# One priority table, a single mask product and token mixing ahead of channel tiles in a blockwise-sparse attention + MLP-mixer kernel whose instruction order is planned at trace time

## The chip, the core and the metric

The kernel runs on one core of one Trainium2 chip. Its time is the device time of one execution in microseconds (us). A profiled execution is one run taken by the hardware profiler; its span runs from the first to the last instruction of the core.

## What is computed

Attention over 4 batches x 8 heads, 768 positions, head width 64, with a mask made of 32 x 32 blocks (neighbours, first and last block row and column, three drawn blocks per row); then a mixer layer over the 4 batches. Cut to what matters:

```python
scores = where(mask, q @ k.T / sqrt(64), -1e9)        # per batch and head, 768 x 768
attn   = softmax(scores) @ v                           # x: 4 x 768 x 512 (heads side by side)
h      = relu(x.T @ w_tok1) @ w_tok2                   # token mixing, 768 -> 256 -> 768
u      = x + h.T
out    = u + relu(u @ w_ch1) @ w_ch2                   # channel mixing, 512 -> 1536 -> 512
```

## The kernel before, in words

**Tiles.** Two heads form a pair; 16 pairs, four to a batch. A pair's 768 queries are cut into three thirds of 256 (index t), and each third has three key steps of 256 (index jj). One (p, t) is called a third here. For each step TensorE makes the transposed scores (line 764), ScalarE the exponential into the SBUF tile `et` (line 777), and TensorE multiplies the exponentials with the values (line 889), 24 matmuls a third, into one PSUM bank. A column of ones in the values gives the row sums; VectorE divides (lines 903 and 904) and writes `x`. The maximum is not subtracted.

**The mask.** In the first five pairs (`p < NT0`, NT0 = 5) 24 more contraction rows add a large negative number to masked scores: four matmuls of 88 rows a step. From pair 5 on the scores are made without it, two heads side by side in the array (64 rows each), 12 matmuls for a whole third, and VectorE multiplies the exponentials by a 0/1 mask (line 794). `CUTS` says how a third is cut for that: one product for steps 0 and 1, one for step 2.

**Getting q and k transposed.** Pairs 1 to 7 by TensorE (line 705), pairs 8 to 15 by DMA transposes from SyncE (line 665), both after loads that GpSimd issues (line 326).

**The mixer.** A batch's token mixing comes in two halves (two pairs each): 12 matmuls (line 970), a relu, 12 matmuls (line 992), three additions (line 1000), a DMA transpose of the sum (line 949). The first batch does it pair by pair, with TensorE transposes (lines 1024, 1046, 1068). Channel mixing: 96 matmuls a batch into 24 relus (lines 1104; 933 on ScalarE or 935 on VectorE), then 72 into six output rows (line 1132), each ended by an addition (line 1144) and a DMA to HBM.

**What sets the order.** Nothing is left to a scheduler. While the program is traced, class `Planner` plays all engines against a clock with assumed costs. TensorE's work comes as streams, each with a priority (lower goes first): scores 0, products with the values 1, transposes `TRP` = 2, the first batch's token mixing `TOKP` = 1.5, the other batches' token mixing 3, channel mixing 4. At each step the first stream whose inputs are there and whose PSUM bank is free emits one instruction. VectorE and ScalarE take from one list of waiting operations the ready one with the lowest `prio`: division 1, evacuations 0.9 or 2, relayouts 2 or 3, token sums and output sums 3, relu 4, mask product 5, exponentials 0. ScalarE leaves another operation alone if it would end more than `GRACE` after the next exponential can start. Engines run in program order, so an instruction that is placed too early blocks its engine.

**Banks.** PSUM has eight banks. In the later phase six belong to scores (three pairs), one (6) and one (7) to all else; `lend` says when a score bank may be lent: only if the time a borrower holds it (`HOLD`), is over before the next third's scores are expected, plus `LATER`.

**The clock.** `START` is the planner's time at the first scores; loads are planned on the same clock from constants.

Of the kernel before, what the change touches and what calls it, by code (L numbers as in the profile page):

```python
# [10 lines left out]
I32 = mybir.dt.int32  # L11
I64 = mybir.dt.int64
PLAN = False
AF = mybir.ActivationFunctionType
ALU = mybir.AluOpType

# [34 lines left out]
class Planner:  # L51
# [6 lines left out]


    PE_LAT, SEM = 180.0, 50.0  # L60
    GRACE = 0.0
    tight = 40e3
    trace = None

# [84 lines left out]
    def step(self):  # L149

        nxt = []
        moved = False
        if self.free_at["pe"] <= self.now:
            for s in self.streams:
                while s[3] is None or (callable(s[3]) and s[3]()):
                    s[3] = next(s[2], False)
                if s[3] is False or callable(s[3]):
                    continue
                cost, deps, tags, emit, done = s[3]
                t = self.when(deps, tags)  # L160
                if t is None:
                    continue
                if self.now < self.tight:

                    t += 300.0 if 1.5 < s[0] < 2.5 else 100.0 if s[0] == 1 else 0.0
                if t <= self.now:
                    s[3] = None
                    emit()
                    if self.trace is not None:
                        self.trace.append((self.now, "pe", s[0], cost))  # L170
                    self.free_at["pe"] = self.now + cost
                    if done is not None:
                        done.t = self.now + cost + self.PE_LAT + self.SEM
                    s[3] = next(s[2], False)
                    moved = True
                    break
                nxt.append(t)
            self.streams = [s for s in self.streams if s[3] is not False]
        else:
            nxt.append(self.free_at["pe"])  # L180
        for eng in ("act", "dve", "sp"):
            if self.free_at[eng] > self.now:
                nxt.append(self.free_at[eng])
                continue
            best, exp_at = None, 1e18
            if eng == "act":
                for o in self.ops:
                    if o[0] == 0 and o[2] == ("act",):
                        t = self.when(o[4], o[8])
                        exp_at = min(exp_at, 1e18 if t is None else max(t, self.now))  # L190
            for o in self.ops:
                prio, num, engines, cost, deps, emit, done, lat, tags = o
                if eng not in engines:
                    continue
                if eng == "act" and prio > 0 and self.now + cost["act"] > exp_at + self.GRACE:
                    continue
                t = self.when(deps, tags)
                if t is None:
                    continue
                if t <= self.now:  # L200
                    if best is None or (prio, num) < best[:2]:
                        best = o
                else:
                    nxt.append(t)
            if best is not None:
                prio, num, engines, cost, deps, emit, done, lat, tags = best
                self.ops.remove(best)
                emit(eng)
                c = cost[eng]
                if self.trace is not None:  # L210
                    self.trace.append((self.now, eng, prio, c))
                self.free_at[eng] = self.now + c
                done.t = self.now + c + lat + self.SEM
                moved = True
        if moved:
            return True
        later = [t for t in nxt if t > self.now]
        if not later:
            return False
        self.now = min(later)  # L220
        return True
# [3 lines left out]
def kernel(  # L225
# [20 lines left out]
    NV = 4  # L246
    NR = 4
    NET = 3
    NPE = 8
    NT0 = 5  # L250
    TOKP = 1.5
    TRP = 2

    sb1 = ctx.enter_context(tc.tile_pool(name="sb1", bufs=1))
    sbw = ctx.enter_context(tc.tile_pool(name="sbw", bufs=2))
# [256 lines left out]
    for hd in range(2):  # L512
        first_evac(vcopy, "k", 2, 4, hd, kt1)
    bandrows = free(indf[:, :], 0, [[0, 2], [1, S]])
    START = 5.7 * US
    P.now = START
    for eng in P.free_at:
        P.free_at[eng] = START
# [113 lines left out]
    def relayout(p):  # L632
        lays = {}
        for nm in ("k", "q", "v") if p >= NT0 else ("v",):
            raw = raws.pop((nm, p))
            arr = arrive.pop((nm, p))

            def emit(eng, nm=nm, raw=raw):
                if nm == "v":
                    nc.vector.tensor_copy(out=vaug[p % NV][:, :, :, 0:64], in_=raw)  # L640
                else:
                    lay = sbw.tile([128, NC, 2, D], BF16, tag=f"{nm}lay", bufs=2, name=f"{nm}lay{p}")
                    nc.vector.tensor_copy(
                        out=lay[:, :, :, :], in_=raw.rearrange("p h c d -> p c h d")
                    )
                    lays[nm] = lay

            deps = [arr]
            if nm == "v" and p >= NV:
                deps.append(pv_done[p - NV])  # L650
            if nm != "v" and p >= NT0 + 2:
                deps.append(qT_there[p - 2, 1])
            if nm != "v" and p >= NPE:
                deps.append(all_loaded)
            lays[nm + "ev"] = P.op(("dve",), {"dve": 320.0}, deps, emit, prio=2 if nm != "v" else 3)
            copied[nm, p] = lays[nm + "ev"]
        va_there[p] = lays["vev"]
        return lays
# [14 lines left out]
    def transposes(p):  # L673
# [15 lines left out]
        for nm, bufs, there in (("k", ktb, kT_there), ("q", qtb, qT_there)):  # L689
# [25 lines left out]
            if p >= NT0:  # L715
                def evac(eng, buf=bufs[p % NV], box=box):
                    copy = nc.scalar.copy if eng == "act" else nc.vector.tensor_copy
                    copy(out=buf[:, 0, :], in_=box["t"][:, :, :].rearrange("p c s -> p (c s)"))

                ev = P.op(  # L720
                    ("dve", "act"), {"dve": 555.0, "act": 740.0}, [last, mask_there], evac, prio=2
                )
                for hd in range(2):
                    alias(there[p, hd], ev)
                alias(rel, ev)
                continue
            for hd in range(2):
                def evac(eng, hd=hd, buf=bufs[p % NV], box=box):
                    i = box["t"][64 * hd : 64 * hd + 64, :, :].rearrange(
                        "p (h c) s -> p h c s", h=2  # L730
                    )
                    o = buf[0:64, :, :].rearrange("p h (c i s) -> p h c i s", c=3, i=2)[:, :, :, hd, :]
                    copy = nc.scalar.copy if eng == "act" else nc.vector.tensor_copy
                    copy(out=o, in_=i)

                ev = P.op(("dve",), {"dve": 550.0}, [last], evac, prio=0.9)
                alias(there[p, hd], ev)
                if hd == 1:
                    alias(rel, ev)

    def alias(a, b):
        a.same_as = b
# [9 lines left out]
    units = [(p, t) for p in range(NP) for t in range(3)]  # L752
    et_rel = {u: Ev() for u in units}
    VISIT = 3
    CUTS = ((0, 1), (2,))

    def scores(s, bank, done, rel, exps):
        p, t, jj = s
# [29 lines left out]
        for group in CUTS:  # L788
            if group[-1] != jj:
                continue  # L790

            def cut(eng, lo=group[0], n=len(group)):
                et = ets[p, t][:, lo : lo + n, :, :, :].rearrange("k j i h q -> k (j i) h q")
                nc.vector.tensor_tensor(  # L794
                    out=et, in0=et,
                    in1=free(mask[:, 2 * lo, 256 * t : 256 * t + 256], 0,
                             [[S, 2 * n], [0, 2], [1, 256]]),
                    op=ALU.mult,
                )

            ev = P.op(("dve",), {"dve": 158.0 + 537.0 * len(group)},
                      [exps[x] for x in group] + [mask_there], cut, prio=5)
            for x in group:
                alias(et_there[p, t, x], ev)

# [4 lines left out]
        return [k_first[int(jj > 0)], q_first[t], e2_first[t]]  # L810

    queue = deque(steps)
    UNSEEN, LATER = 2500.0, 1800.0
    HOLD = {"pm": 1600.0, "po": 1800.0, "ch1": 1800.0, "ch2": 4000.0}

    def lend(tag):
        if not queue:
# [54 lines left out]
    def pv_stream():  # L872
        for s in steps:
# [3 lines left out]
            def emit(s=s, done=done):  # L877
# [33 lines left out]
                        op=ALU.mult,  # L911
                    )

                ev = P.op(("dve",), {"dve": 610.0}, [done], norm, prio=1)
                alias(rel, ev)
                alias(x_there.setdefault((p, t), Ev()), ev)

# [41 lines left out]
    def tok(b, g):  # L959
        deps = [x_there[2 * g + 4 * b + i, h] for i in range(2) for h in range(3)] + [tok1_there]  # L960

        urgent = 3
        box = {}
        last, rel = Ev(), Ev()
        for t in range(2):
# [122 lines left out]
    def ch(b):  # L1088
# [4 lines left out]
        for cc in range(12):  # L1093
            for sh in range(2):
                last, rel, pbox = Ev(), Ev(), {}
                for dmc in range(4):
# [18 lines left out]
                    yield 162.5, deps, tags, emit, last if dmc == 3 else None  # L1115
                ev = relu_op(
                    lambda cc=cc, sh=sh: box["rc"][:, cc, 384 * sh : 384 * sh + 384],
                    pbox["pm"][:, 0:384], [last], 4,
                )
                alias(rel, ev)  # L1120
                rc_there[cc, sh] = ev
# [4 lines left out]
        for sc, lo, n in parts:  # L1126
# [30 lines left out]
                    in_=o[:, 0:n],  # L1157
                )

            alias(rel, P.op(("dve",), {"dve": dve_psum(n)}, [last], fin, prio=3))  # L1160
        alias(rc_rel, last)


# [27 lines left out]
    P.stream(TRP, tr_stream())  # L1191
    P.stream(TOKP, tok_first_stream(range(3)))
    P.stream(-1, tok_first_stream((3,)))
    P.stream(3, tok_stream((1, 2, 3)))
    P.stream(4, ch_stream())
    P.stream(1.8, mask_stream())

# [77 lines left out]
```

## Time and profile before

| what | us |
|---|---|
| median of 14 runs | 252.07 (251.58 to 257.71) |
| the profiled execution, as timed | 252.0 |
| its span | 250.3 |
| TensorE matmuls / VectorE / ScalarE / GpSimd busy | 242.4 / 164.7 / 176.5 / 49.4 |
| mask products: 33 of two steps, 33 of one step | 40.2 and 22.6 |
| exponentials, 144 | 137.1 |

The page gives one execution. "Busy" is the time in which an engine had at least one instruction under way; matmuls overlap their successors, so a matmul's own length (193 ns for one with 65 columns) is much more than the distance to the next (about 30 ns). For TensorE this text therefore reads distances between starts. An idle time is followed by what ended it, as in `<-DVE x`. The granted TensorE clock was 1.000 through the whole span.

### The profile page before, as it was taken

To read this page: it belongs to the slowest core of one execution; us is meant where nothing else is said; L and a number is where in the kernel's file an instruction comes from. 1 tells how busy PE (TensorE), PEld (TensorE's weight loads), DVE (VectorE), ACT (ScalarE), POOL (GpSimd) and SP (SyncE) were. 2 spreads that over 40 slices of the span, in tenths; PEclk is the share of its full clock that TensorE was granted. 3 is DMA by queue.
4 is the path that set the end of the run, shared out by engine and by line. 5 is a ranking of instruction groups with operands and counts; after the bars stand their busy time and mean duration, and the time that the engine had idled before them with its cause. 6 is when DMAs were issued, how large, how long until landed. Compare 5 with 4: busy or idle time off the path is not lost.

```text
span 250.3 us, 6580 instructions
## 1 busy us (share of the span) xinstructions
PE 242.4 (97%) x2788; PEld 163.0 (65%) x2807; DVE 164.7 (66%) x339; ACT 176.5 (71%) x225; POOL 49.4 (20%) x86
## 2 busy tenths in 40 slices
PE   8899999999999989999999999999999999999994
PEld 3689999966675557566765556666775665566444
DVE  5984885758697997988647687878795655200222
ACT  5999999998967777488669778589978820377000
POOL 8935888657600000000000000000000000000000
PEclk9999999999999999999999999999999999999999
DMA  7999999999976950663031452150006024300132
GB/s 163 162 219 202 203 207 201 205 201 203 199 119 120 169 133 24 92 162 65 0 65 34 74 87 63 47 148 0 3 0 65 3 84 93 138 3 0 42 118 94
DMA packets 42461, 26.35 MB, mean 105 GB/s; under 512 B 23680, under 2 KB 38800, under 8 KB 42432
## 3 DMA queue, kind: packets, MB, share of 16 engines
q0 software_dynamic: 15104, 12.98, 33.0%
q1 hardware_dynamic: 26784, 12.56, 22.7%
q8 instruction: 22, 0.36, 0.6%
q10 hardware_dynamic: 544, 0.39, 0.5%
q14 instruction: 7, 0.06, 0.1%
HBM read 26.74 MB, written 6.29 MB: 132 GB/s over the span
## 4 chain that ended last, share of the span: by engine, by line
PE 88%; DMA 4%; POOL 3%; DVE 2%; issue 1%; ACT 1%; POOLq 0%
PE banks L1132 25%; PE banks L1104 24%; PE banks L764 15%; PE banks L889 13%; DMA w_tok<-in_moe_w_tok_dram 4%; PE banks L970 3%; PE banks L992 3%; PE banks L705 1%; PE banks L1024 1%; PE banks L1046 1%; POOL vraw L326 1%; POOL kraw L326 1%; POOL qraw L326 1%; PE banks L1068 1%; ACT et L777 1%
## 5 line engine op out<-in xcount | busy, mean ns | idle before, releaser
L777 ACT ACTIVATE et<-banks 128x1024 bf16<-128x1024 f32 x144 | 137.1, 1024 | 24.5 <-PE banks L764 24.0
L1132 PE MATMUL banks<-w_ch,rc 128*128 128x512 bf16 (+2 forms) x293 | 67.7, 362 | 2.2 <-DVE x L904 1.0
L1104 PE MATMUL banks<-uT,w_ch 128*128 128x384 bf16 x384 | 68.5, 326 | 0.0
L794 DVE TENSOR_TENSOR et<-et,mask 128x2048 bf16<-128x2048 bf16 x66 | 61.2, 952 | 3.2 <-ACT et L777 3.1
L764 PE MATMUL banks<-qtb,ktb 64*128 64x256 bf16 (+1 forms) x576 | 54.3, 271 | 0.4 <-ACT et L777 0.4
L889 PEld LDWEIGHTS <-et 128*128 128x128 bf16 x1152 | 45.7, 97 | 10.2 <-DVE et L794 2.1
L889 PE MATMUL banks<-vaug,et 128*128 128x65 bf16 x1152 | 50.3, 193 | 0.3
L933 ACT ACTIVATE rc<-banks 128x384 bf16<-128x384 f32 x71 | 34.4, 495 | 23.0 <-PE banks L1104 22.4
L1104 PEld LDWEIGHTS <-w_ch 128*128 128x128 bf16 x384 | 35.7, 98 | 22.1 <-issue 1.3
L1132 PEld LDWEIGHTS <-rc 128*128 128x128 bf16 x312 | 27.7, 97 | 27.6 <-issue 3.5
L764 PEld LDWEIGHTS <-ktb 64*128 64x128 bf16 (+1 forms) x576 | 31.9, 95 | 15.2 <-issue 12.1
L1144 DVE TENSOR_TENSOR o<-banks,x 128x512 f32<-128x512 f32 x23 | 15.8, 687 | 30.7 <-PE banks L1132 30.6
L903 DVE RECIPROCAL recip<-banks 128x4 f32<-128x4 f32 x48 | 8.7, 181 | 27.8 <-PE banks L889 26.6
L904 DVE TENSOR_TENSOR x<-banks,recip 128x256 bf16<-128x256 f32 x48 | 20.4, 424 | 1.7
L935 DVE TENSOR_SCALAR rc<-banks 128x384 bf16<-128x384 f32 x25 | 13.8, 554 | 7.3 <-PE banks L1104 7.1
L1000 DVE TENSOR_TENSOR x<-banks,x 128x512 bf16<-128x512 f32 x18 | 11.4, 683 | 3.1 <-PE banks L992 3.1
L970 PE MATMUL banks<-x,w_tok 128*128 128x256 bf16 x72 | 10.0, 273 | 0.0
L992 PE MATMUL banks<-a_t,w_tok 128*128 128x256 bf16 x72 | 9.2, 273 | 0.3 <-DVE a_t L935 0.3
L992 PEld LDWEIGHTS <-w_tok 128*128 128x128 bf16 x72 | 7.9, 126 | 0.9 <-issue 0.4
L970 PEld LDWEIGHTS <-w_tok 128*128 128x128 bf16 x72 | 6.6, 98 | 2.4 <-issue 0.8
L326 POOL DMA_DIRECT2D vraw<-in_v_dram x10 | 7.4, 742 | 2.5 <-DVE recip L903 1.2
L326 POOL DMA_DIRECT2D kraw<-in_k_dram x9 | 6.6, 729 | 4.3 <-DMA w_tok<-in_moe_w_tok_dram 2.7
(94 smaller groups left out, 132.3 us busy)
## 6 DMA issues: line engine op xcount, KB each, us to landing
out_dram<-o SPq DMA_DIRECT2D x23, 256.0 KB, 2.0
w_ch<-in_moe_w_ch_dram POOLq DMA_DIRECT2D x8, 384.0 KB, 9.8
vraw<-in_v_dram POOLq DMA_DIRECT2D x10, 192.0 KB, 7.3
kraw<-in_k_dram POOLq DMA_DIRECT2D x9, 192.0 KB, 8.8
qraw<-in_q_dram POOLq DMA_DIRECT2D x9, 192.0 KB, 7.3
w_tok<-in_moe_w_tok_dram POOLq DMA_DIRECT2D x2, 384.0 KB, 10.8
qf<-in_v_dram POOLq DMA_DIRECT2D x4, 192.0 KB, 7.8
klay_first<-in_k_dram POOLq DMA_DIRECT2D x2, 192.0 KB, 8.3
```

What stands on the lines that cost most here:

```text
L326: nc.gpsimd.dma_start(out=raw, in_=APx(src, 2 * p * S * D, [[NC * D, 128], [S * D, 2], [1, NC * D]]),)
L764: nc.tensor.matmul(out=ps[:, hd, 256 * i : 256 * i + 256], lhsT=ktb[n][rows, h, 256 * jj + 128 * i : 256 * jj + 128 * i + 128], rhs=qtb[n] ...
L777: nc.scalar.activation(out=ets[p, t][:, jj, :, :, :].rearrange("k i h q -> k h i q"), in_=ps.rearrange("k h (i q) -> k h i q", i=2), func= ...
L794: nc.vector.tensor_tensor(out=et, in0=et, in1=free(mask[:, 2 * lo, 256 * t : 256 * t + 256], 0, [[S, 2 * n], [0, 2], [1, 256]]), op=ALU.mult,)
L889: nc.tensor.matmul(out=po[:, hd, c, :], lhsT=et[:, jj, i, hd, 128 * c : 128 * c + 128], rhs=va[:, hd, 2 * jj + i, 0:65], start=(jj == 0 an ...
L904: nc.vector.tensor_tensor(out=free(xs[b][:, pb // 2, 2 * t, 128 * (pb % 2) : 128 * (pb % 2) + 128], 0, [[64, 2], [256, 2], [1, 64]],), in0 ...
L933: nc.scalar.activation(out=o(), in_=i, func=AF.Relu)
L970: nc.tensor.matmul(out=box["pm"][:, t, :], lhsT=w_tok1[:, sc, 128 * t : 128 * t + 128], rhs=xs[b][:, g, sc, :], start=(t == 0 and sc == 0) ...
L992: nc.tensor.matmul(out=ubox["pm"][:, i, :], lhsT=w_tok2[:, t, :, 2 * s2 + i], rhs=a_t[:, t, :], start=(i == 0 and t == 0), stop=(i == 1 an ...
L1104: nc.tensor.matmul(out=pbox["pm"][:, 0:384], lhsT=w_ch1[:, dmc, 128 * cc : 128 * cc + 128], rhs=st[b]["uT"][:, dmc // 2, 3 * sh : 3 * sh + ...
L1132: nc.tensor.matmul(out=pbox["pm"][:, 0:n], lhsT=box["rc"][:, cc, 128 * sc : 128 * sc + 128], rhs=w_ch2[:, cc, lo : lo + n], start=(cc == 0 ...
L1144: nc.vector.tensor_tensor(out=o[:, :].rearrange("p (g e) -> p g e", g=2), in0=pbox["pm"][:, :].rearrange("p (g e) -> p g e", g=2), in1=st[ ...
```

## The change

All numbers of the planner are put into one table `KN` and several are different; one of them picks another cut for the mask product. The diff, cut to its core:

```diff
+KN = dict(
+    tokp=2.5, trp=2.6, toks=1.2, later=1400.0, unseen=1500.0, h_pm=1200.0, h_po=1800.0,
+    h_ch1=1400.0, h_ch2=3500.0, relayk=0.8, relayv=4.6, fin=2.1, relu=0.85, cut=5.0, norm=0.6,
+    add=3.0, ev2=2.0, ev4=3.3, grace=400.0, m1=0.0, m2=150.0, nt0=5, cuts=2, xbar=8,
+)
-    GRACE = 0.0
+    GRACE = KN["grace"]
-                    t += 300.0 if 1.5 < s[0] < 2.5 else 100.0 if s[0] == 1 else 0.0
+                    t += KN["m2"] if s[0] == KN["trp"] else KN["m1"] if s[0] == 1 else 0.0
-    TOKP = 1.5
-    TRP = 2
+    TOKP = KN["tokp"]
+    TRP = KN["trp"]
-    START = 5.7 * US
+    START = 6.5 * US
-    CUTS = ((0, 1), (2,))
+    CUTS = (((0,), (1,), (2,)), ((0, 1), (2,)), ((0, 1, 2),), ((0,), (1, 2)))[KN["cuts"]]
-    UNSEEN, LATER = 2500.0, 1800.0
-    HOLD = {"pm": 1600.0, "po": 1800.0, "ch1": 1800.0, "ch2": 4000.0}
+    UNSEEN, LATER = KN["unseen"], KN["later"]
+    HOLD = {tag: KN["h_" + tag] for tag in ("pm", "po", "ch1", "ch2")}
-    P.stream(3, tok_stream((1, 2, 3)))
+    P.stream(KN["toks"], tok_stream((1, 2, 3)))
```

The `prio` numbers of VectorE's and ScalarE's operations are read from the table in the same way: relayouts of q and k 2 to 0.8, of v 3 to 4.6, evacuations 0.9 to 2.0 and 2 to 3.3, division 1 to 0.6, relu 4 to 0.85, output sum 3 to 2.1; token sums (3) and mask product (5) stay. The mask product of a third becomes one operation over three steps. NT0 and the number of pairs transposed by TensorE are the same numbers as before. Nothing that is computed changes, and TensorE's instructions are the same in number and kind; their order is not.

## The prediction, made before the changed kernel ran

> **What bounds the kernel now.** I read the page's busy shares first, then the chain that ended last, then TensorE's timeline.
>
> ```profile
> PE 242.4 (97%) x2788; PEld 163.0 (65%) x2807; DVE 164.7 (66%) x339; ACT 176.5 (71%) x225; POOL 49.4 (20%) x86
> ...
> PE 88%; DMA 4%; POOL 3%; DVE 2%; issue 1%; ACT 1%; POOLq 0%
> ```
>
> TensorE carries 88% of the chain. The Trainium skill (Perfetto Trace Analysis, "Identifying the Most-Contended Engine") warns that matmul busy share doesn't show how near a kernel is to its bound, and says to take weight-load busy share: here 65%, which would leave a third of the span, some 85 us, to be had by a better order. The trace decides, by distances between starts. The chain in order of time has
>
> ```profile
> 100.85 2.16 PE banks L1132 x10
> ...
> 123.52 1.31 PE banks L992 x12
> ...
> 215.95 15.60 PE banks L1104 x96
> ```
>
> (start, length, what), so 0.216, 0.109 and 0.1625 us a matmul. A third's 12 scores take 0.86 with the step into them, 24 value products 0.73 (0.0305 each), a step of the first five pairs 0.436, a small transpose or first-batch token matmul 0.056. Sum: 45 x 0.436 + 33 x 0.86 + 1152 x 0.0305 + 384 x 0.1625 + 288 x 0.216 + 2.65 (the last row's small pieces) + 144 x 0.109 + 204 x 0.056 = 237.4 us. From the first scores (6.18) to the last matmul (247.2) are 241.0 us. So TensorE is full; only some 3 us are idle, and no order can win more. That is the ceiling, not 85.
>
> Where are they? I compared, from one third's scores to the next, the elapsed time with the work in between. Most of the 32 intervals agree within 0.02 us. One that doesn't:
>
> ```profile
> 88.98 0.83 PE L764 MATMUL banks<-qtb,ktb 64*128 64x256 bf16 x12
> 89.74 0.60 PE L1132 MATMUL banks<-w_ch,rc 128*128 128x512 bf16 x2
> 90.18 0.89 PE L889 MATMUL banks<-vaug,et 128*128 128x65 bf16 x24
> 91.80 0.81 PE L1132 MATMUL banks<-w_ch,rc 128*128 128x512 bf16 x2 [0.73 <-DVE x L904]
> 92.54 0.83 PE L764 MATMUL banks<-qtb,ktb 64*128 64x256 bf16 x12
> ```
>
> Value products started at 90.18 end after 0.73 at 90.91; the next channel row waits until the division has freed their bank, at 91.80: 0.89 idle (one of its three matmuls is missing in the record). By the same sum: 0.49 from 96.19 (relu of a token half), 0.22 from 102.94, 0.09 from 109.86, 0.43 from 113.65 (mask product), 0.46 from 138.24 (division), 0.12 in two others. **Together 2.7 us after pair 5 has begun.** The other waits are in the first 19 us.
>
> **One mask product instead of two.**
>
> ```profile
> L794 DVE TENSOR_TENSOR et<-et,mask 128x2048 bf16<-128x2048 bf16 x33 | 40.2, 1219 | 3.2 <-ACT et L777 3.1
> ...
> L794 DVE TENSOR_TENSOR et<-et,mask 128x1024 bf16<-128x1024 bf16 x33 | 22.6, 685 | 0.0
> ```
>
> Two steps take 1219 ns, one 685: 534 a step and 151 fixed. Three steps then take 1.75 us (an estimate from these rows; at least that, at most the 1.90 of both). VectorE saves 33 x 0.151 = 5.0 us. In the new order 16 more channel relus are VectorE's (41 for 25, 554 ns each: +8.9), so its busy time rises to about 168 us, and ScalarE loses 16 x 0.495 = 7.9. Neither sets the end, so both count nothing by themselves.
>
> What counts is that the values must wait longer. From the start of a third's scores: 0.49 to the first exponential (134.49 to 134.98), 2.85 for three, 0.05, product, 0.1. Before, the last step was ready after 0.49 + 2.85 + 0.05 + 0.69 + 0.1 = 4.2 us, now all of it after 5.24. Here the skill speaks against the change: Perfetto Trace Analysis, "Optimizing Scalar/DVE Operations", says that grouping pays where the engine is saturated, and that where VectorE isn't but makes others wait, operations should be broken up. VectorE is at 66%. By the rule, with values where they were (TensorE work between scores and values 4.4 to 4.9 us in some 20 thirds), each would wait some 0.6: +12 us. By the new order it doesn't: values come later too. Summing TensorE's work between scores and values at the prices above gives 5.32 to 5.49 us in ten thirds, 5.5 to 9.6 in the others. All cover 5.24, ten with a margin of only 0.08 to 0.25. I take the order's sum.
>
> **The new priorities and lending.** The order shows what they do after pair 5: a third's 24 values run unbroken (before, mostly 16 and 8 with channel work between); 24 of 48 accumulators for values lie in lent score banks (5 before), so channel rows wait less for a division. Unbroken or not, they cost the same: 0.73. I went through the places of the new order where an instruction follows closely on what frees its bank or makes its input. None of the old waits is left, two new ones are. (a) Values of pair 12, second third: after the last of 12 token matmuls TensorE has 4 channel rows' matmuls, scores, 6 token and 1 channel matmul, 0.86 + 0.86 + 0.65 + 0.22 = 2.6 us; VectorE in that time ends a division (0.65), the token relu (0.69) and the product (1.75), 3.1 to 3.2 with hand-over: 0.5 idle. (b) Pair 7, last third: three products stand in VectorE's queue with an output sum and a division between; 0.2 short. Cost 0.7; the bounds are 0.3 (the old waits were often shorter than such a sum) and 1.2.
>
> SyncE's queue: the transpose of batch 1's first half moves ahead of pair 8's q and k (1.3 us each). Those land by about 81 us and are read at 90: hidden. Batch 1's second half is read about 5.6 us after its issue; the row of such a transpose shows 5.2 to landing: covered by 0.4, up to 0.4 more if SyncE is late. GpSimd's loads are the same in number, with some homes exchanged from pair 5 on, and nothing ahead of them changed. The last was issued at 67.3, landed some 8 us later and is read after 110, so this costs nothing.
>
> So after pair 5: -2.7 + 0.7 = -2.0 us.
>
> **START and the first token matmul.** This part loses. `START` moves the planner's scores 0.8 us later against its own estimate of loads, so it believes loads to be there sooner relative to TensorE's work.
>
> ```profile
> 17.77 0.60 PE L764 MATMUL banks<-qtb,ktb 88*128 88x256 bf16 x4
> 18.21 0.41 PE L889 MATMUL banks<-vaug,et 128*128 128x65 bf16 x8
> 18.83 0.40 PE L1024 MATMUL banks<-x,w_tok 128*128 128x128 bf16 x4 [0.21 <-DMA w_tok<-in_moe_w_tok_dram]
> ...
> DMA to landing us min/median/max: 9.9/9.9/9.9
> ```
>
> The first token weights (issued at 8.93, landing after 9.9) come at 18.83, and the first matmul that reads them waits for just that. No load ahead of them changes, so they will again. In the new order one such matmul stands ahead of a score step and 16 values that now run ahead of it: 0.436 + 0.488 = 0.92 us. TensorE gets there at about 17.8 (also after new waits for pair 1's q, landing at 10.28, and pair 2's k, at 13.4, which this wait swallows), stands until 18.83, and has 0.92 us of work more ahead than before. From 20 to 49 us TensorE shows no wait for ScalarE, so nothing absorbs it: **+0.9 us** (bounds 0.2, if ScalarE's queue turns out to rule there, and 1.0).
>
> **Sum.** -2.0 + 0.9 = -1.1 against the profiled execution's 252.0 (span 250.3 and 1.7 around it): span 249.2, time 250.9. The median before, 252.07, is the same within 0.1.
>
> **Rivals.**
> - The early delay is absorbed, because exponentials and TensorE are nearly balanced in the first 50 us (ScalarE 98% busy from 20 to 50). Then 250.9 - 0.9 = 250.0. Against it: no idle on TensorE there. 0.13.
> - Idle is only moved: new waits of 1.2 to 2.2 us that my sums miss, at transposes and in bank hand-overs, together with the early 0.9 give 251.4 to 252.4. This is also the case that the table doesn't do what it says, as relus go to VectorE. 0.22.
> - Slower: the long product starts late. VectorE is in the middle of a relu or sum (0.55 to 0.69) when the third exponential ends; nothing can overtake, and the values stand at the head of TensorE's queue. With lateness 0.3 in the ten tight thirds and the five next (margin 0.3) the shortfalls add to 1.0, nearly the whole gain; with 0.4 to 2.4: 253.3. It decides from about 0.3 on. For it: VectorE gets the 16 relus; against: in the new order the product follows right on the last exponential in most thirds. 0.12.
>
> **How the numbers follow.** Likeliest 0.53: 250.9, of its own 250.2 to 251.6. A measurement of this kernel can tell about 0.3% from no change, 0.76 us: faster is below 251.3. That is most of the likeliest case, and all of the first rival: 0.66. Same 0.22, slower 0.12. The range, 249.8 to 252.4, takes in the first rival, most of the second and the bounds of the waits, and leaves out the slow one.
>
> **What would show it.** TensorE idle about 1.0 us before 18.83 with the token weights as releaser, and the score step after it at about 18.9; pair 5's first scores near 54.1 as before, with 6 fewer channel matmuls ahead of them (0.97 us, which hides the delay there); from there to the last batch's 96 channel matmuls 2 us less idle, those starting near 214.9 (before 215.95); the product at about 1750 ns x33; waits of channel rows for the division gone. Wrong would be: products above 1.9 us, TensorE idle before values in more than five thirds, or a first-token wait that doesn't move the later starts.

## The result, and the profile after

| | before | after |
|---|---|---|
| median, us (runs) | 252.13 (48, with those shown above) | 250.56 (10, 249.98 to 251.25) |
| ratio, 95% interval | | 0.9939 [0.9924, 0.9955] |
| profiled execution, as timed / span | 252.0 / 250.3 | 250.6 / 248.9 |

The change gains 0.6%, 1.6 us. Ratios, here and below, take the undisturbed executions alone, against the kernel before as timed on the same chip. The page of the kernel after, busy shares, chain and the groups that the change touches (the changed kernel's line numbers are 5 or 6 higher):

```profile
PE 242.1 (97%) x2788; PEld 163.1 (66%) x2807; DVE 170.3 (68%) x321; ACT 170.1 (68%) x210; POOL 49.7 (20%) x86
...
PE 90%; ACT 4%; DMA 2%; DVE 1%; issue 1%; SPq 0%; DVEq 0%
...
L1138 PE MATMUL banks<-w_ch,rc 128*128 128x512 bf16 (+2 forms) x293 | 65.7, 362 | 1.1 <-issue 0.2
L800 DVE TENSOR_TENSOR et<-et,mask 128x3072 bf16<-128x3072 bf16 x33 | 57.8, 1752 | 1.7 <-ACT et L783 1.5
...
L941 DVE TENSOR_SCALAR rc<-banks 128x384 bf16<-128x384 f32 x41 | 22.2, 553 | 5.3 <-PE banks L1110 4.3
```

The three-step product takes 1752 ns, 33 times, and 41 channel relus are VectorE's. TensorE's busy time stands where it stood. The list of what TensorE waited for is short now (waiting line, releaser: us in all, times, longest):

```profile
PE banks L469 <- ACT qlay_first L461: 1.0, 1, 1.0
PE banks L394 <- DVE one L387: 1.0, 1, 1.0
PE banks L770 <- ACT et L783: 0.3, 1, 0.3
PE banks L1138 <- issue: 0.2, 1, 0.2
```

Before, it had channel rows waiting for the division (1.0 us) and token products for a relu (0.3). Both are gone, and no wait for another engine after pair 5 is named in their place. The list is not complete: the comparison of starts, as in the prediction, finds two places more, 0.45 us in pair 12 and 0.12 in pair 9 (shown further below). TensorE's timeline in pair 12 (start, length):

```profile
154.31 0.83 PE L770 MATMUL banks<-qtb,ktb 64*128 64x256 bf16 x12
155.07 0.64 PE L998 MATMUL banks<-a_t,w_tok 128*128 128x256 bf16 x4
155.54 0.38 PE L1138 MATMUL banks<-w_ch,rc 128*128 128x512 bf16 x1
155.87 0.38 PE L998 MATMUL banks<-a_t,w_tok 128*128 128x256 bf16 x2
156.36 0.90 PE L895 MATMUL banks<-vaug,et 128*128 128x65 bf16 x24
```

Two token matmuls need 0.22, so the values at 156.36 start 0.27 later than TensorE could. A further 0.11 lies ahead of the token matmuls at 155.87; what caused it was not settled. VectorE at the same time:

```profile
153.62 0.42 DVE L910 TENSOR_TENSOR x<-banks,recip 128x256 bf16<-128x256 f32 x1
153.96 0.68 DVE L941 TENSOR_SCALAR a_t<-banks 128x512 bf16<-128x512 f32 x1
154.56 1.75 DVE L800 TENSOR_TENSOR et<-et,mask 128x3072 bf16<-128x3072 bf16 x1
```

Division, token relu, product, one behind the other: the product ends at 156.31, and the values follow at 156.36. These 0.27 are wait (a) of the prediction. The chain of waits, in order of time, has near its end

```profile
214.59 15.60 PE banks L1110 x96
```

The last batch's 96 channel matmuls start at 214.59, before at 215.95: 1.36 sooner, the whole difference of the spans (1.4).

**Two numbers that split every run.** One is the start of the last score step of the first five pairs, TensorE's 45th: it tells how late the front is. Before it was at 49.00, after at 49.73. The other is TensorE's idle time after pair 5: from pair 5's first scores to the last third's, the elapsed time less the work in between at the prediction's prices. Before it was 2.85, after 0.76. So the front lost 0.73 and the rest gained 2.09: 250.3 + 0.73 - 2.09 = 248.9, the span measured. All runs of the study, split in this way:

| run | median, us | ratio, 95% interval | 45th step | idle after pair 5 | sum | span |
|---|---|---|---|---|---|---|
| before | 252.13 | | 49.00 | 2.85 | | 250.3 |
| before again | 251.68 | 0.9999 [0.9984, 1.0015] | 48.97 | 2.85 | 250.3 | 250.3 |
| after | 250.56 | 0.9939 [0.9924, 0.9955] | 49.73 | 0.76 | 248.9 | 248.9 |
| after again | 250.81 | 0.9953 [0.9937, 0.9969] | 50.01 | 0.76 | 249.2 | 249.2 |
| after, START 5.7 | 250.9 | 0.9962 [0.9946, 0.9977] | 49.38 | 0.76 | 248.6 | 248.6 |
| after, token weights planned later | 250.03 | 0.9932 [0.9920, 0.9945] | 49.10 | 0.77 | 248.3 | 248.3 |
| after, two products | 255.48 | 1.0149 [1.0124, 1.0173] | 48.93 | 5.99 | 253.4 | 253.4 |
| before, one product | 255.65 | 1.0150 [1.0132, 1.0167] | 48.60 | 5.96 | 253.0 | 253.9 |
| after, old lending | 251.8 | 0.9992 [0.9973, 1.0012] | 49.66 | 1.98 | 250.1 | 250.1 |
| before, new priorities | 252.69 | 1.0027 [1.0007, 1.0047] | 49.36 | 2.46 | 250.3 | 250.3 |
| the same and GRACE | 253.49 | 1.0061 [1.0044, 1.0078] | 49.54 | 3.51 | 251.5 | 251.5 |
| the same and one product | 251.74 | 1.0001 [0.9978, 1.0025] | 49.70 | 1.98 | 250.1 | 250.1 |
| after, GRACE 0 | 264.13 | 1.0493 [1.0443, 1.0543] | 49.37 | 9.47 | 257.3 | 259.9 |
| after, two edits | 250.33 | 0.9933 [0.9900, 0.9965] | 50.18 | 0.48 | 249.1 | 249.1 |

The sum is 250.3 plus the differences of both columns from before. It meets the span within 0.1 in all but two runs: with one product in the kernel before, 0.9 lies behind the last third's scores; with GRACE at 0, 2.6, of which 2.40 is a wait of the last batch's channel matmuls for a transpose. The two columns lie in stretches that don't overlap, so the two parts of the prediction can be judged apart. They say nothing of the time outside the span: with the new priorities alone the span is that of the kernel before, but 2.0 us of the profiled execution (252.31) lie outside it, for 1.7 before.

### The profile page after: what moved, and what is told of

It is laid out like the page before. It is cut to its first block, busy times and chain, and to the rows that moved or that the text cites. A ratio compares the mean times of both kernels' runs of the same rounds, so it can differ in the third digit from the quotient of the medians.

```text
span 248.9 us, 6575 instructions
## 1 busy us (share of the span) xinstructions
PE 242.1 (97%) x2788; PEld 163.1 (66%) x2807; DVE 170.3 (68%) x321; ACT 170.1 (68%) x210; POOL 49.7 (20%) x86
## 4 chain that ended last, share of the span: by engine, by line
PE 90%; ACT 4%; DMA 2%; DVE 1%; issue 1%; SPq 0%; DVEq 0%
PE banks L1110 26%; PE banks L1138 24%; PE banks L770 16%; PE banks L895 13%; ACT et L783 4%; PE banks L976 3%; PE banks L998 3%; DMA qf<-in_q_dram 2%; PE banks L711 1%; PE banks L1052 1%; PE banks L1030 1%; DVE et L800 1%; PE banks L1074 1%; ACT qlay_first L461 0%; PE banks L469 0%
## 5 line engine op out<-in xcount | busy, mean ns | idle before, releaser
L1138 PE MATMUL banks<-w_ch,rc 128*128 128x512 bf16 (+2 forms) x293 | 65.7, 362 | 1.1 <-issue 0.2
L800 DVE TENSOR_TENSOR et<-et,mask 128x3072 bf16<-128x3072 bf16 x33 | 57.8, 1752 | 1.7 <-ACT et L783 1.5
L895 PEld LDWEIGHTS <-et 128*128 128x128 bf16 x1152 | 43.6, 97 | 6.6 <-issue 1.1
L895 PE MATMUL banks<-vaug,et 128*128 128x65 bf16 x1152 | 46.7, 193 | 0.1
L939 ACT ACTIVATE rc<-banks 128x384 bf16<-128x384 f32 x55 | 26.8, 492 | 22.1 <-PE banks L1110 21.6
L941 DVE TENSOR_SCALAR rc<-banks 128x384 bf16<-128x384 f32 x41 | 22.2, 553 | 5.3 <-PE banks L1110 4.3
L976 PE MATMUL banks<-x,w_tok 128*128 128x256 bf16 x72 | 9.5, 273 | 0.1
L615 POOL COPY mask<-maskb 128x240 bf16<-128x240 bf16 (+1 forms) x18 | 7.4, 478 | 0.0
```

The lines of the kernel that those rows point to most:

```text
L800: nc.vector.tensor_tensor(out=et, in0=et, in1=free(mask[:, 2 * lo, 256 * t : 256 * t + 256], 0, [[S, 2 * n], [0, 2], [1, 256]]), op=ALU.mult,)
L895: nc.tensor.matmul(out=po[:, hd, c, :], lhsT=et[:, jj, i, hd, 128 * c : 128 * c + 128], rhs=va[:, hd, 2 * jj + i, 0:65], start=(jj == 0 an ...
L939: nc.scalar.activation(out=o(), in_=i, func=AF.Relu)
L941: nc.vector.tensor_scalar(out=o(), in0=i, scalar1=0.0, scalar2=None, op0=ALU.max)
L976: nc.tensor.matmul(out=box["pm"][:, t, :], lhsT=w_tok1[:, sc, 128 * t : 128 * t + 128], rhs=xs[b][:, g, sc, :], start=(t == 0 and sc == 0) ...
L1138: nc.tensor.matmul(out=pbox["pm"][:, 0:n], lhsT=box["rc"][:, cc, 128 * sc : 128 * sc + 128], rhs=w_ch2[:, cc, lo : lo + n], start=(cc == 0 ...
```

## The experiments

The theory that stood after the result: after pair 5 the gain comes from the order that all parts of the table make together, and the front's loss is real and hidden by nothing. Rivals: one part alone (priorities, merge, lending, GRACE) makes the gain; the front's loss comes from the first token matmul, as predicted, or from how the first loads happen to land. Each expectation stands as it was put on record before its run.

**Both kernels again**, without an edit, show what repeats.

> The kernel before, unchanged, for a second trace of its first 20 us and of its idle time. If the loads at the start vary from run to run, the first token matmul starts at another time than 18.83 us or the second part of q arrives at another time than 6.3 us, while the idle time of TensorE after pair 5 stays at 2.7 to 2.9 us, since the order is fixed. If the idle time after pair 5 is chance, it differs by more than 0.5 us. Time 252.0.

> The changed kernel, unchanged. Theory: idle time of TensorE from pair 5's first scores to the last third's is 0.8 us as in its first trace (0.45 of it before the values of pair 12, second third). The early delay depends on when the first token weights land: at 18.8 us they cost 0.9, at 16.6 nothing. Rival: the 1.0 us by which q's second part came later in the first trace belongs to the change, and is seen again here. Time 250.6 by the theory with early weights, 251 with late ones.

Measured: idle after pair 5 repeats to 0.01 us (2.85 and 2.85, 0.76 and 0.76). The front does not: the 45th step came 1.04 later in this pair of profiles, 0.73 in the first. In the second profile of the changed kernel TensorE stands in the front at another place:

```profile
11.14 0.51 PE L711 MATMUL banks<-ident,qraw 128*128 128x128 bf16 x6 [0.83 <-DMA qraw<-in_q_dram]
11.48 0.60 PE L770 MATMUL banks<-qtb,ktb 88*128 88x256 bf16 x4
```

Pair 1's q landed at 11.1 (10.3 in the first profile), and its transposes now stand ahead of a score step, pair 0's fifth. In the kernel before that score step came first.

**START back.**

```diff
-    START = 6.5 * US
+    START = 5.7 * US
```

> The changed kernel with START = 5.7 again. From pair 4 on its order is that of the changed kernel; before that pair 1's q and pair 2's k are turned later, and the first token matmul stands behind a score step and 16 values as in the kernel before. If START costs 0.9 us by the wait for the first token weights, this is 0.9 faster than the changed kernel where they land at 18.8 and 0 to 0.2 faster where they land at 16.6. If the earlier turning of q and k fills idle time of TensorE near 9 to 12 us (its rival), START = 6.5 is a gain and this is 0.5 to 0.8 slower.

Measured: 250.9, as good as the changed kernel's 250.81 on the same chip; idle after pair 5 again 0.76. The order after pair 4 is the same. From the fifth score step to the 45th it takes 39.33, with START at 6.5 38.50; the fifth step comes sooner in exchange (10.05). By these medians and the equal idle time, START is not what made the gain, and not what lost the front.

**The planner believes the first token weights 0.9 us later**, so that the first token matmul stands behind one more score step and 16 values.

```diff
-        tok1_there.t = landing(t, S * DT * 2).t
+        tok1_there.t = landing(t, S * DT * 2).t + 900.0
```

> The changed kernel, with the planner's arrival of the first token weights put 0.9 us later, and nothing else. Early turning of q and k stays; the first token matmul moves behind a score step and 16 values. From pair 4 on the order is that of the changed kernel. If the wait for those weights costs, 0.9 faster than the changed kernel with weights at 18.8, the same with weights at 16.6. If the early delay is all q's late part, the same in any case.

Measured: the first token matmul moved from 18.23 to 18.93, and from the fifth score step to the 45th it takes 38.57 for 38.50. So its place cost nothing, with the weights landing at 16.66 and 17.70 in the two. The front was 0.6 sooner than in the changed kernel's profile because this run's first loads landed sooner (below). The median, 250.03, is lower than the changed kernel's, but the intervals overlap.

**One part undone or done alone: the cut of the product.** The changed table with the old cut, then the old kernel with the new cut:

```diff
-    ... nt0=5, cuts=2, xbar=8,
+    ... nt0=5, cuts=1, xbar=8,
```

> The changed kernel with two mask products a third again (cuts=1), all else as changed. If the merge itself pays (one fixed cost of 0.15 us less a third), this loses little, 0 to 1 us, and half of the gain after pair 5 stays. If the breaking-up rule is right here, it is faster than the changed kernel. My theory: the planned order fits only its own set of numbers; places in its order where channel rows and value accumulators follow closely on an output sum or a division add to 4 to 6 us of idle time after pair 5 against 0.8: time 253.5 to 255.5.

```diff
-    CUTS = ((0, 1), (2,))
+    CUTS = ((0, 1, 2),)
```

> The kernel before with one mask product a third and nothing else. If the merge carries the gain, 250.5 to 251.5. By my theory it alone costs: the values come later, bank hand-overs then meet the output sums, and the places in its order add to about 5 us of idle time after pair 5 against 2.8, and one transposed token half is read too early at the end (up to 1.3): time 254 to 255.5. Without any move of the values by the planner it would be 264.

Measured: both lose 1.5%, with idle times of 5.99 and 5.96. In the changed table with two products, values wait 1.4 us in one place, and channel rows 1.6 us in three, for an output sum on VectorE. The old order with the long product pays at pair 9 for what the rule cited in the prediction would break up (TensorE's timeline):

```profile
107.99 0.40 PE L764 MATMUL banks<-qtb,ktb 64*128 64x256 bf16 x4 [0.47 <-ACT et L777]
108.90 0.40 PE L764 MATMUL banks<-qtb,ktb 64*128 64x256 bf16 x4 [0.52 <-ACT et L777]
110.70 1.50 PE L889 MATMUL banks<-vaug,et 128*128 128x65 bf16 x24 [1.40 <-DVE et L794]
112.01 2.30 PE L1104 MATMUL banks<-uT,w_ch 128*128 128x384 bf16 x7
```

Scores wait for exponentials to free their banks, then the values wait 1.40 for the product. Counted from start to start, these waits make only 2.7 of the 4.39 us lost there. The 24 values then take 1.31 to the next start instead of 0.73, and the channel matmuls behind them run slowly too. The table by windows (length, PE, PEld, DVE, ACT and POOL busy, granted TensorE clock, DMA share, GB/s) says why:

```profile
107.00:110.70 3.70, 1.31 (x14) 0.52 (x13) 2.36 (x2) 3.70 (x6) 0.00 (x0) 0.99 1.05 224
110.70:114.00 3.30, 3.30 (x31) 2.29 (x32) 1.73 (x4) 1.39 (x2) 0.00 (x0) 0.50 0.39 88
114.00:118.00 4.00, 4.00 (x52) 2.59 (x51) 2.72 (x7) 3.59 (x5) 0.00 (x0) 0.99 0.02 4
```

The low clock lasts from 110.63 to 114.05. In these 3.4 us TensorE does the work of 1.7, so 1.7 us come on top of the waits. All four executions of this kernel were granted 0.993 over the span, as one such stretch makes it (3.41 x 0.5 of 253.9 is 0.0067).

**Lending undone.**

```diff
-    later=1400.0, unseen=1500.0, h_pm=1200.0, h_po=1800.0, h_ch1=1400.0, h_ch2=3500.0
+    later=1800.0, unseen=2500.0, h_pm=1600.0, h_po=1800.0, h_ch1=1800.0, h_ch2=4000.0
```

> The changed kernel with the lending rule's numbers as before (unseen, later, hold). If lending of score banks to values is what removed the waits for divisions, this has idle time after pair 5 of 2 us or more and gives back at least 1.2. If the priorities and the merged product do it, under 1.5 us of idle time: the sum over its order gives about 1.5 to 2.0 against 0.8, so 251.2 to 251.8.

Measured: idle 1.98, in four places (0.74, 0.34, 0.22, 0.49), the first with token products that wait 0.57 for a relu; the time is that of the kernel before. The new lending is worth 1.22 us of the 2.09, in this table.

**Priorities alone**, in the kernel before (relayouts 0.8 and 4.6, evacuations 2.0 and 3.3, division 0.6, relu 0.85, output sum 2.1).

> The kernel before with the new priorities of VectorE's and ScalarE's operations and nothing else (two products, old lending, GRACE, START and streams). If the priorities make the gain, 250.0 to 250.8. The sum over its order gives about 2.0 to 2.5 us of idle time after pair 5 against 2.8, and up to 0.8 more in the first 15 us: 251.5 to 252.5, no change to be told.

Measured: idle 2.46 for 2.85, but the front 0.36 later; the two cancel, and the span is that of before. The median is 0.3% slower, part of which lies outside the span (see above).

**GRACE, and then the merge, on top of the priorities** (old lending, old stream priorities, START 5.7; the second differs from the first in one number). Both were made from the changed kernel by putting the old values into its table, with all of which the planner emits the program of the kernel before; here they stand as edits of that kernel:

```diff
-    GRACE = 0.0
+    GRACE = 400.0
```

> The kernel before with two parts of the table: the new priorities of VectorE's and ScalarE's operations and GRACE = 400 (two products a third, old lending, old streams, START 5.7). Theory 1 (no part pays by itself; the order that all of them make together does): TensorE's idle time after pair 5 stays at 2.5 to 3.8 us, as in the kernel before (2.85) and with the priorities alone (2.46), and the time at 252.0 to 253.3. Theory 2 (GRACE, by letting ScalarE take relus and sums off VectorE, removes the waits for VectorE whatever the cut): idle 0.8 to 1.5 us, time about 250.8.

```diff
-    CUTS = ((0, 1), (2,))
+    CUTS = ((0, 1, 2),)
```

> The same with the single product over three steps (priorities, GRACE = 400 and the merge; old lending, old streams, START 5.7). Theory 1 expects an intermediate result: the merge stands in an order that leaves room for it, but the old lending keeps some waits for VectorE: idle after pair 5 1.3 to 2.2 us, time 250.9 to 251.8. Theory 2 expects what it expects of the run without the merge, 250.8, since the merge only takes 5 us of VectorE's busy time. A third theory, that the lending rule is what makes the gain, expects no gain here: idle 2.5 us or more, 252 or more.

Measured: without the merge 3.51 idle and 0.6% slower, with it 1.98 and as fast as before. From pair 5 on the second has the same order as the changed kernel with old lending, and the same idle time; so the priorities of the streams and START do nothing there. In this order the merge is worth 1.53 us, where alone it cost 3.1. Without the merge VectorE is late: channel rows wait 1.0 us in two places for an output sum to free their bank, values 0.5 for a division. Which single move in the order takes which wait away was not settled. Nor was the changed table run with the old priorities, or the new lending or GRACE alone in the kernel before: what a part is worth is known for the tables above only.

**GRACE undone in the changed kernel.**

```diff
-    add=3.0, ev2=2.0, ev4=3.3, grace=400.0,
+    add=3.0, ev2=2.0, ev4=3.3, grace=0.0,
```

> The changed kernel with GRACE back at 0, everything else as changed. Theory 1: without it ScalarE leaves relus and additions alone, VectorE becomes late for the long products, and the values wait for them: by the order's own distances some 9 to 14 us of new idle time on TensorE, of it about 3 at one wait of values for a product, 3 at a channel matmul that waits for a transpose of SyncE's, and 4 to 5 in the last batch; time 260 to 264. Theory 2 (the table's single numbers hardly matter once the products are merged): within 1 us of the changed kernel, 250 to 252.

Measured: 4.9% slower. The list of TensorE's waits begins with

```profile
PE banks L895 <- DVE et L800: 4.2, 2, 2.8
PE banks L1110 <- DMA uT<-x: 3.6, 2, 2.4
```

Values wait for the long product, and channel matmuls for the transposes of token sums that VectorE finished late. The longest lies behind two divisions, three token sums and an output sum that all stand ahead of the product on VectorE. The clock adds to it again: 0.50 from 112.34 to 115.75 us, behind 2.78 and 1.18 us of waiting. The profiled execution was granted 0.992 over the span, the four others 0.980 to 0.987, which would be two or three such stretches instead of one (an estimate: one is 3.41 x 0.5 of 260, 0.0066). That fits a median 2.5 above the profiled 261.66.

**A version that might beat both**: the later token weights, and the relu of wait (a) given to ScalarE, so that the product starts sooner.

```diff
-        a_there = relu_op(lambda: a_t[:, :, :], box["pm"][:, :, :], [last], urgent)
+        a_there = relu_op(lambda: a_t[:, :, :], box["pm"][:, :, :], [last], urgent,
+                          ("act",) if (b, g) == (2, 1) else ("dve", "act"))
```

(`relu_op` hands that tuple to `P.op` as the engines allowed.)

> The changed kernel with two edits: the relu of the last token half of batch 2 may only go to ScalarE (VectorE then has the product of pair 12's second third 0.7 us sooner), and the planner believes the first token weights 0.9 us later. If the 0.45 us that values wait in pair 12 come from the relu in front of that product, as the prediction has it, idle after pair 5 falls from 0.76 to about 0.3 us, and the time from 250.0 to 250.8 (the changed kernel and the one with the later token weights) to 249.6 to 250.3. If the wait comes from the product's own length, or ScalarE's exponentials fall behind by its 0.8 us relu, idle stays at 0.7 to 1.0 and the time at 250.0 to 250.8.

Measured: idle 0.48, of it 0.17 at the place that had 0.45. VectorE's timeline there:

```profile
154.07 0.42 DVE L910 TENSOR_TENSOR x<-banks,recip 128x256 bf16<-128x256 f32 x1
154.48 1.76 DVE L800 TENSOR_TENSOR et<-et,mask 128x3072 bf16<-128x3072 bf16 x1
```

No relu in between; the product now follows the third exponential (ended at 154.44), and the values follow the token matmuls without a wait. Wait (a) is confirmed in its cause. The 0.11 ahead of the two token matmuls is still there. The time, 250.33, can't be told from the changed kernel's by these intervals; the profiled execution had the latest front of all (50.18). The lowest times fit a gain of 0.3 (249.62, for 249.98 and 250.16 of the changed kernel and 249.95 with the token weights alone), but that is not shown to be a better kernel.

## Why the prediction was right, and where it was not

**The ceiling** held for the part that was found by comparing intervals: TensorE's idle time after pair 5 was 2.85 of the 250.3, and no version won more than 2.37 of it. The prediction's other way to the ceiling, the sum of 237.4, has a slip. It takes 288 channel row matmuls at full width and adds the last row's small pieces; but of the 312 weight loads on `rc` 36 are those pieces (24 of 128 columns, 12 of 256), which leaves 276. The sum is then 234.8, and some 6 us are idle, about 3 of them ahead of pair 5, where ScalarE sets the pace (below). "No order can win more" than 3 was therefore not shown for the whole kernel. The weight-load share would have promised 85 us; it is 63 to 66% in the slowest versions and the fastest alike.

**The merged product**: 1.75 was estimated, 1752 ns measured. VectorE's busy time became 170.3 (about 168 predicted) and ScalarE lost 6.4, not 7.9. The groups moved as the sum said (products -5.0, channel relus +8.5 on VectorE and -7.7 on ScalarE); the rest is small groups and how far records overlap. Neither counts, as the prediction said. The rule to break such operations up was weighed against the order's sum. Taken alone it is right in direction: in the old table the merge costs 3.1 us of idle time and 1.5% (the rule's sum, with every value where it was, was 12; the planner moves most of them).

In the changed order TensorE's work between scores and values covered the longer product in eight of the ten tight thirds. It failed to in two, in both because of a product that VectorE began late, so the third rival came there in small. One is wait (a). The other is pair 9's first third, the tightest:

```profile
108.03 1.75 DVE L800 TENSOR_TENSOR et<-et,mask 128x3072 bf16<-128x3072 bf16 x1
109.83 0.82 PEld L895 LDWEIGHTS <-et 128*128 128x128 bf16 x24 [0.26 <-DVE et L800]
```

The third exponential had ended at 107.87, but VectorE was copying v. The values start at 109.89, 5.32 after their scores (104.57); TensorE was free 0.09 earlier. The margins were also 0.1 smaller than the prediction had them: its 0.86 for scores counts the step into them, which lies ahead of their start, while 5.24 is counted from that start.

**After pair 5**: -2.0 predicted, -2.09 measured. Wait (a) was sized 0.5; 0.27 came at the place and with the cause named, and 0.11 more close by. Wait (b), 0.2, did not come. The transpose of batch 1's second half was covered and cost nothing. The late product of pair 9, which the prediction put in its third rival, makes most of the 0.12 there. The old waits are gone. This step was right in mechanism and size, though that the 0.7 and the measured 0.76 agree so well is in part luck.

**START and the first token matmul**: this step failed, and that its size came out near (0.9 predicted, 0.73 measured) is luck. Predicted was that TensorE gets to the first token matmul at about 17.8, stands until the weights land at 18.83, and loses 0.9. In the profile after:

```profile
17.80 0.60 PE L770 MATMUL banks<-qtb,ktb 88*128 88x256 bf16 x4
18.23 0.22 PE L1030 MATMUL banks<-x,w_tok 128*128 128x128 bf16 x1
18.71 0.60 PE L770 MATMUL banks<-qtb,ktb 88*128 88x256 bf16 x4 [0.26 <-ACT et L783]
```

The token matmul runs at once. Its weights, issued at 8.93 as before, landed after 7.7 us and not 9.9; in the runs listed they land between 16.3 and 18.8. And the wait that follows is for an exponential. "No load ahead of them changes, so they will again" took one landing for a constant. With the matmul at this early place the latest landing seen is 18.18 (old lending): it ran at 18.23, and the score step behind it again waited for an exponential (0.16). A landing at 18.8 in this order was not seen.

The second mistake was "nothing absorbs it". ScalarE's timeline of the kernel after, from its cast of the second half of the first q:

```profile
7.37 0.62 ACT L461 CAST qlay_first<-qf 128x512 bf16<-128x512 f32 x1 [1.75 <-DMA qf<-in_q_dram]
...
9.22 31.36 ACT L783 ACTIVATE et<-banks 128x1024 bf16<-128x1024 f32 x33 [0.19 <-PE banks L770]
```

and of the kernel before:

```profile
6.33 0.62 ACT L456 CAST qlay_first<-qf 128x512 bf16<-128x512 f32 x1 [0.71 <-DMA qf<-in_q_dram]
...
8.18 11.31 ACT L777 ACTIVATE et<-banks 128x1024 bf16<-128x1024 f32 x12 [0.19 <-PE banks L764]
19.70 21.16 ACT L777 ACTIVATE et<-banks 128x1024 bf16<-128x1024 f32 x22 [0.21 <-PE banks L764]
```

33 exponentials without a gap, 0.950 each: ScalarE rules the front. (Both timelines are cut at 40 us.) Before, the wait of 18.83 for the token weights shows as a gap of 0.21. The fifth score step to the 45th are 40 exponentials, 38.0 us; measured 38.50 after, 38.83 before, and 38.54 in the second profile of the kernel before, where the weights landed at 18.32 and left no gap. Behind the fifth step the new order costs nothing. So the first rival, that exponentials absorb the early delay, had the mechanism right; its 250.0 leaves out what is lost ahead of the fifth step.

The fifth step comes 1.06 later, the stretch behind it is 0.33 shorter: the whole 0.73 arises ahead of it. The cast waited for its load until 7.37, before until 6.33, and in both kernels the fifth step comes 3.84 to 3.86 after a late cast (from 6.3 on), unless pair 1's q is later. That last condition is the new order's: the fifth step then starts 0.4 after that landing (11.48 for 11.1 in the second profile).

With early casts (5.5 to 5.7) the 45th step came at 48.93 and 49.10 in two runs with the new order of the front, and at 48.60 in one with the old. So the prediction's lower bound, "0.2, if ScalarE's queue turns out to rule there", was the right branch, and the rest of the 0.7 to 1.0 is landing times and one wait for a landing. How much of it the order causes in the mean is left open: by the fifth step's lateness against its cast, 0.0 in the first profile and 1.0 in the second. That loads land later in the changed kernel as a rule is not shown either: the casts lie at 5.5 to 7.6 with START 6.5 and at 5.5 to 6.6 with START 5.7.

`START` itself was judged by the wrong thing. With the new priorities at START 5.7 the fifth step to the 45th takes 39.3 to 39.5 (four runs), at 6.5 38.5 to 38.9 (seven runs), with the old priorities at 5.7 38.5 to 38.8 (three). The new priorities cost this stretch 0.8, and the later START takes that back.

**"Token mixing ahead"** was given no cost and no gain. With the other batches' stream at priority 3 again and all else as changed, the planner emits the same program, instruction for instruction, so nothing was there to measure.

**The signs**: pair 5's first scores at 53.89 (about 54.1 predicted), the 96 matmuls at 214.59 (214.9). The sign named first, TensorE idle for the token weights ahead of 18.83, did not come. The time is 250.56 for 250.9: the front and the rest each a little better.

## What to carry to other kernels

Where an order is planned at trace time, the parts of a table can't be priced one by one: the merge alone, and the table without the merge, each cost 1.5%, and together they gain 0.6%. Judge a whole order by one sum over distances between starts of the bounding engine. Take the landing times of the first loads into it as a spread, not as a constant. Give an operation's added length a cost only where the work between its cause and its reader is shorter, and count both from the same start.

## What the runs showed of the hardware that was not expected

A long stretch of waits costs TensorE twice. With one product in the kernel before, TensorE was busy for 1.09 of the 3.41 us from 107.22 to 110.63, and its clock was then granted at 0.50 for 3.41 us. With GRACE at 0 it was busy for 0.90 of the 3.41 us from 108.93 to 112.34, with the same result. In that run two other stretches of 3.41 us (from 170.36 and from 221.56), one with a wait of 1.40 and one with most of a wait of 2.40, were busy for 1.70 each and left the clock at 1.00. The Trainium skill (TensorE: Matmul & The Clock Gate, "What's actually happening") has the clock halved after an idle window of about 3.4 us; here a window with a third of work in it was enough, and one with half was not.

Loads at the same place of a queue, issued at the same time, landed up to 2.5 us apart from run to run (the first token weights, 16.3 to 18.8), while the idle time behind pair 5 repeated to 0.01 us.
